# Loads a batch ahead behind a spread that GpSimd issues, query transposes two units earlier, first scores in four visits

## The chip, the cores and the metric

The kernel runs on one core of one Trainium2 chip. Its time is the device time of one execution in microseconds; the figure shown is the median of the runs made. The profile is of one further execution of the same program.

## The reference

Two layers in a row. The first is attention with projected keys and values (8 batches, 8 heads, 1024 tokens, head size 64, 64 projected positions), the second a gated feed-forward network on the 8192 rows that result (512 wide, 1536 hidden).

```python
k_proj = einsum('ks,bhsd->bhkd', E, k);  v_proj = einsum('ks,bhsd->bhkd', F, v)
attn = softmax(q @ k_proj.T / 8)
x = (attn @ v_proj) with heads side by side: 8192 x 512
gate = 1 / (1 + exp(-(x @ w_gate)));  val = x @ w_val
out = (gate * val) @ w_out
```

## The kernel before, in words

All weights stay on the chip. The work goes batch by batch: while the network runs on batch b (two blocks of 512 tokens, each in three thirds of the hidden width, hence six "units" per batch), the attention of batch b + 1 is done in between. All large products are of Strassen's form, seven for eight, and therefore come as chains of small groups: `g_chain` (L1771) and `v_chain` (L1800) once per unit, `o_chain` (L1451) once per block, three units apart. Each chain accumulates in two PSUM banks; ACT copies a bank into the other one as a start (`seed`, L1675) or evacuates it, DVE adds and multiplies.

**What attention of one batch needs**, in the order of its steps:

- K and V (`load_k`, `load_v`, L401 and L411) and Q (`load_q`, L429) are loaded by GpSimd's queue (POOL) from HBM, turned into bf16 on the way, into one buffer each (`KV[0]`, `KV[1]`, `Qb`). A load waits until the buffer's last reader is done: for Q these are the four DMA transposes, for K and V the matmuls of `kv`.
- `next_kv` (L1999): `kv` projects both on PE, `keep_kd` (L896) copies the keys with ACT into `kpd` and lets SP issue one DMA transpose into `kpD` (L910).
- `transpose_q` (L866): SP issues four DMA transposes, r = 0 to 3, two heads each, from `Qb` into `qT` (L870).
- `sc_visit` (L1193): scores of some r on PE, then the exponentials on ACT into `eT`. `den_visit` (L1209): sums of them on PE (`den8`), reciprocals on DVE (`rec`, L977), then `spread`.
- `spread` (L1146): SP writes the reciprocals to DRAM (`rd`, 128 KB, L1149) and, when that has landed, reads them back in four DMAs that repeat each row over 64 partitions (`xu<-rd`, L1165, 512 KB each). The first two are round 0 and serve the first two r, the other two are round 1.
- `xo_visit` (L1201): attention times values on PE, then on DVE the product with the spread, into `xT` (`scaled`, L1182). `xs_sums` makes the sums that the next batch's chains need.

`o_chain` ends in `ost`: ACT evacuates a first quarter early in the chain (`evac`, L1447, shown as L382 with tile `ost`), and at its end SP stores four pieces of 256 KB (`stored`, L1436, L1441). The next block's `evac` may write `ost` only when those stores have landed. After `evac` on ACT come further copies, among them `seed` for the chains that PE works on.

**What sets the order.** For batch 0 and the start of the next the order is written out by hand (`todo`, `put`). From L1992 on, calls of `add` only collect tasks, and `arranged` (L53) makes one order of them: it simulates the engines with fixed costs and takes, among what could start, the task with the earliest due time. A group of matmuls has a goal; unit u of batch b lies at `when(6b + u)`, 9.9 us apart (PACE, L1993), counted from the start of that part. A DMA is counted as 0.6 us of SP or 0.85 us of POOL (L40) and lands after 3.0 us, or after `t` (26 for a load, 8 for a spread). `tie` names keys that a task is to come after, in the plan only: no semaphore is waited on for it. `pad` (default 3.0, SP's tasks alone) is added to what a task waits for, in the plan only. What the program really waits for follows from the keys in `r`, `w` and `x` (L149 to L186). Each engine's queue is then worked off strictly in the order made.

In the main loop (L2022 to L2062), b is the batch of the network and n the attention of batch b + 1. Before the change, batch b starts with `load_k(b + 2)` and `load_v(b + 2)`; for b = 1 visits come one unit later (`late_`). Scores of r = 0, 1 come in unit 0, those of 2, 3 and the sums in unit 1; after them, tied to the spread, `transpose_q` for batch b + 2 and `load_q(b + 3)`, the latter with a real wait for the spread. `next_kv(b + 2)` and the first output visit come in unit 3, the second in unit 4.

Of the kernel before, what the change touches and what calls it, by code (L numbers as in the profile page):

```python
# [116 lines left out]
class Plan:  # L117
# [28 lines left out]
        self.tasks.append(self.open)  # L146
        self.open = None

    def add(self, eng, fn, r=(), w=(), x=(), dma=None, t=None, tie=(), pad=3.0):  # L149
        if self.tasks is not None:  # L150
            self.note(eng, (eng, fn, tuple(r), tuple(w), tuple(x), dma), t, tie, pad)
            return None
        op = Op()
        op.eng, op.fn, op.dma, op.need = eng, fn, dma, False
        op.sem, op.val = None, 0
        deps = {}

        def dep(o, raw):
            if o is op:
                return  # L160
            if o.eng == eng and o.dma is None:
                if eng == "PE" or (eng != "POOL" and not raw):
                    return
            deps[id(o)] = o

        for k in r:
            for o in self.writers.get(k, ()):
                dep(o, True)
        for k in tuple(w) + tuple(x):
# [63 lines left out]
def bass_linformer_attn__then__ffn_glu_sigmoid_kernel(  # L233
# [11 lines left out]
    B = q.shape[0]  # L245
# [6 lines left out]
    with contextlib.ExitStack() as es:  # L252
# [139 lines left out]
        wg_v = moe_w_gate.rearrange("(i p) f -> p i f", p=P)  # L392
        wv_v = moe_w_val.rearrange("(i p) f -> p i f", p=P)

        def load(o, i, w, sem, r=()):
            add("POOL", lambda e: e.dma_start(o, i), r=r, w=w, dma=sem, t=26.0)

        def turned():
            return [("qT", r) for r in range(NR)]

        def load_k(b, after=()):  # L401
            n = 0
            load(
                KV[n][:, :, :],
                k[b].rearrange("h (p t) d -> p h (t d)", t=NT),
                [("KV", n, 0), ("KV", n, 1)],
                f"KV{n}",
                r=(turned() if b >= 2 else []) + list(after),
            )

        def load_v(b):  # L411
            n = 1
            load(
                KV[n][:, :, :],
                v[b].rearrange("h (p t) d -> p h (t d)", t=NT),
                [("KV", n, 0), ("KV", n, 1)],
                f"KV{n}",
            )

        def load_kv_heads(n, src, R):  # L420
# [5 lines left out]
                f"KV{n}{R}",  # L426
            )

        def load_q(b, after=()):  # L429
            load(  # L430
                Qb[:, :, :],
                q[b].rearrange("h (p t) d -> p h (t d)", t=NT),
                [("Q", hf, R) for hf in range(2) for R in range(2)],
                "Q",
                r=after,
            )

        def load_q_half(b, hf, R):
# [424 lines left out]

            return qt, sc, den, bc, xo

        def transpose_q(tie=()):  # L866
            for r in range(NR):
                add(
                    "SP",
                    lambda e, r=r: e.dma_start_transpose(  # L870
                        qT[:, 2 * r : 2 * r + 2, :].rearrange("p h (t c) -> p (h t) c", c=P),
                        Qb[:, 2 * r : 2 * r + 2, :].rearrange("p h c -> p (h c)"),
                    ),
                    r=[("Q", hf, r // 2) for hf in range(2)],
                    w=[("qT", r)] + [("qT", hf, r // 2, r % 2) for hf in range(2)],
                    dma=f"qT{r}",
                    tie=tie,
                )
# [53 lines left out]
        def attention(b):  # L932
# [213 lines left out]
            def spread():  # L1146
# [4 lines left out]
                    w=[("rd", b)],  # L1151
                    dma="rd",
                    t=2.5,
                    pad=0.0,
                )
                for rnd in range(2):
                    for c in range(2):
                        src = (
                            rd_v[b]
                            .rearrange("(g m) (o c) -> o g m c", g=8, o=1)[:, :, 2 * rnd + c, :]  # L1160
                            .to_broadcast([64, 8, 256])
                        )
                        add(
                            "SP",
                            lambda e, src=src, rnd=rnd, c=c: e.dma_start(  # L1165
                                rb[64 * c : 64 * c + 64, rnd, :, :, :].rearrange(
                                    "p j h c -> p (j h) c"
                                ),
                                src,
                            ),  # L1170
                            r=[("rd", b)],
                            w=[("rb", c, rnd), ("spread", c, rnd)],
                            dma=f"rb{c}{rnd}",
                            t=8.0,
                            pad=0.0,
                        )

            def scaled(r, g, bk):
                n = 2 * r + g
# [256 lines left out]
        def stored(blk, tts):  # L1436
            for tt in tts:
# [4 lines left out]
                    r=[("ost", tt, n) for n in range(2)],  # L1442
                    dma=f"out{tt}",
                    t=3.0,
                )

        def evac(bk, tok, col):  # L1447
# [563 lines left out]
        for n in (1, 2, 3, 4):  # L2011
            xs_sums(2, n)
        next_kv(2, -2.0)
        transpose_q()
        t_sums(4)
        t_sums(1)
        o_chain(1, OA, OC, 0.0, 2.0, sums=False)
        for n in (1, 2, 3, 4):
            xs_sums(3, n)

        load_q(3)
        for b in range(1, B):  # L2022
            n = attention(b + 1) if b + 1 < B else None
            if b + 2 < B:
                load_k(b + 2)
                load_v(b + 2)
            late_ = 1 if b == 1 else 0
            for u in range(6):
                K = 6 * b + u
                t0 = when(K)  # L2030
                if n is not None:
                    if u == late_:
                        n["sc_visit"](t0 - 1.0, (0, 1), (GA, GC, XA, XB))
                    if u == late_ + 1:
                        n["sc_visit"](t0 - 1.0, (2, 3), (GA, GC, XA, XB))
                        n["den_visit"](t0 + 3.0, XA)
                        if b + 2 < B:
                            transpose_q(n["spread_keys"])
                        if b + 3 < B:
                            load_q(b + 3, n["spread_keys"])  # L2040
                    if u == late_ + 3:
                        if b > 1 and b + 2 < B:
                            next_kv(b + 2, t0 - 5.0)
                        n["xo_visit"](t0 - 1.0, (0, 1), (GA, GC, XA, XB))
                        if b == 1:
                            next_kv(3, t0 + 4.0)
                    if u == late_ + 4:
                        n["xo_visit"](t0 - 1.0, (2, 3), (GA, GC, XA, XB))
                        for i in (1, 2, 3, 4):
                            xs_sums(2 * b + 2, i)  # L2050
# [46 lines left out]
```

## Time and profile before

| | |
|---|---|
| median of 3 runs | 571.79 us (567.17 to 573.63) |
| the profiled execution's own time | 564.84 us |
| its span, first to last instruction | 563.1 us |
| granted TensorE clock, mean | 0.967 |
| busy share of the span: PE, DVE, ACT, POOL | 91%, 72%, 62%, 7% |
| DMA over the span | 123 GB/s on average; 36.0% of 16 engines' span from POOL's queue, 33.5% from SP's |

In the profile, times are microseconds from the first instruction; "L870" is line 870 of the kernel. SPq and POOLq are queues in which instructions that issue DMAs stand; the length of such an instruction is the time until the queue goes on, not until the data has landed. Where the queue's timeline merges equal instructions (x4), the length reaches from the first one's start to the last one's end. A line of waits tells which engine stood, at which instruction, and what ended it. Nearly all matmuls have one line (L378) and nearly all ACT copies another (L382), so one goes by tiles: pA and pF are PSUM banks.

### The profile page before, as it was taken

To read this page: it belongs to the slowest core of one execution; us is meant where nothing else is said; L and a number is where in the kernel's file an instruction comes from. 1 tells how busy PE (TensorE), PEld (TensorE's weight loads), DVE (VectorE), ACT (ScalarE), POOL (GpSimd) and SP (SyncE) were. 2 spreads that over 40 slices of the span, in tenths; PEclk is the share of its full clock that TensorE was granted. 3 is DMA by queue.
4 is the path that set the end of the run, shared out by engine and by line. 5 is a ranking of instruction groups with operands and counts; after the bars stand their busy time and mean duration, and the time that the engine had idled before them with its cause. 6 is when DMAs were issued, how large, how long until landed. Compare 5 with 4: busy or idle time off the path is not lost.

```text
span 563.1 us, 11315 instructions
## 1 busy us (share of the span) xinstructions
PE 513.1 (91%) x4668; PEld 402.9 (72%) x4677; DVE 405.3 (72%) x670; ACT 351.5 (62%) x644; POOL 37.0 (7%) x52
## 2 busy tenths in 40 slices
PE   5999998798999969999299992999989999999996
PEld 4545546586788858877188781888768888888885
DVE  3648698477886857959168684677777969795964
ACT  2564736575886737874268670587747866667662
POOL 9210200100100010000100001000000000000000
PEclk9999999799999989999599997899989999999999
DMA  9999999958996993179952399822941172010113
GB/s 167 198 201 192 165 223 171 154 139 133 173 201 127 177 218 73 48 105 115 221 97 76 72 113 214 145 76 42 152 127 38 39 162 74 14 63 31 46 39 112
DMA packets 90307, 69.41 MB, mean 123 GB/s; under 512 B 35088, under 2 KB 82448, under 8 KB 90256
## 3 DMA queue, kind: packets, MB, share of 16 engines
q0 software_dynamic: 33984, 29.89, 36.0%
q1 hardware_dynamic: 56272, 38.81, 33.5%
q8 instruction: 36, 0.59, 0.4%
q14 instruction: 15, 0.12, 0.1%
HBM read 72.88 MB, written 17.56 MB: 161 GB/s over the span
## 4 chain that ended last, share of the span: by engine, by line
PE 76%; SPq 9%; DMA 7%; DVE 3%; ACT 2%; issue 1%; POOL 1%; ACTq 0%; DVEq 0%; POOLq 0%
PE pA L378 42%; PE pF L378 34%; SPq L870 8%; DMA out_dram<-ost 2%; DMA KVs<-in_v_dram 2%; DMA xu<-rd 2%; SPq L1441 1%; ACT pF L1678 1%; DMA kpD<-kpd 1%; DVE xT L1182 0%; DVE hT L1811 0%; ACT ost L382 0%; ACT vsnap L382 0%; DVE xT L816 0%; DVE vsnap L1689 0%
## 5 line engine op out<-in xcount | busy, mean ns | idle before, releaser
L382 ACT ACTIVATE sig<-pA 128x512 f32<-128x512 f32 x126 | 75.1, 596 | 49.5 <-PE pA L378 48.4
L1765 DVE TENSOR_TENSOR sig<-pF,sig 128x512 f32<-128x512 f32 x84 | 57.7, 687 | 66.7 <-PE pF L378 38.6
L1689 DVE TENSOR_TENSOR vsnap<-pF,vsnap 128x512 f32<-128x512 f32 x90 | 61.9, 688 | 25.8 <-PE pF L378 14.5
L1678 ACT ACTIVATE pF<-pA 128x512 f32<-128x512 f32 x99 | 58.0, 588 | 32.8 <-PE pA L378 29.8
L378 PE MATMUL pF<-wO,hT 128*128 128x256 bf16 (+1 forms) x400 | 58.8, 285 | 0.2 <-issue 0.2
L1811 DVE SCALAR_TENSOR_TENSOR hT<-sig,vsnap 128x512 bf16<-128x512 f32 x84 | 56.7, 680 | 1.0
L382 ACT ACTIVATE vsnap<-pA 128x512 f32<-128x512 f32 x84 | 50.1, 596 | 8.3 <-PE pA L378 7.2
L382 ACT ACTIVATE sig<-sig 128x512 f32<-128x512 f32 x84 | 52.5, 630 | 4.0 <-DVE sig L1765 3.6
L378 PE MATMUL pF<-xS,wV 128*128 128x256 bf16 x360 | 54.6, 275 | 0.1
L378 PE MATMUL pA<-xS,gT 128*128 128x256 bf16 x168 | 26.4, 282 | 29.2 <-ACT pF L1678 29.2
L378 PE MATMUL pA<-xT,gT 128*128 128x256 bf16 x336 | 51.9, 278 | 0.0
L378 PE MATMUL pF<-xT,wG 128*128 128x256 bf16 (+1 forms) x257 | 50.4, 317 | 1.6 <-DVE hT L1287 0.8
L378 PE MATMUL pF<-xS,wG 128*128 128x256 bf16 x336 | 51.4, 276 | 0.0
L378 PE MATMUL pA<-xT,vT 128*128 128x256 bf16 x336 | 50.5, 273 | 0.0
L378 PE MATMUL pA<-wT,hT 128*128 128x256 bf16 x360 | 49.5, 275 | 0.0
L382 ACT ACTIVATE sig<-pF 128x512 f32<-128x512 f32 x66 | 39.4, 596 | 15.3 <-PE pF L378 13.4
L378 PEld LDWEIGHTS pF<-wO,hT 128*128 128x128 bf16 x402 | 38.5, 98 | 10.3 <-issue 0.8
L378 PEld LDWEIGHTS pF<-xS,wV 128*128 128x128 bf16 x360 | 34.0, 98 | 10.8 <-issue 3.5
L378 PE MATMUL pF<-xT,wV 128*128 128x256 bf16 (+1 forms) x240 | 41.5, 294 | 0.0
L378 PEld LDWEIGHTS pA<-xS,gT 128*128 128x128 bf16 x168 | 15.5, 99 | 34.0 <-ACT pF L1678 30.6
L1811 DVE SCALAR_TENSOR_TENSOR hT<-sig,pF 128x512 bf16<-128x512 f32 x42 | 28.6, 681 | 14.2 <-PE pF L378 12.4
L378 PEld LDWEIGHTS pA<-wT,hT 128*128 128x128 bf16 x360 | 35.4, 99 | 4.7
(152 smaller groups left out, 901.2 us busy)
## 6 DMA issues: line engine op xcount, KB each, us to landing
out_dram<-ost SPq DMA_DIRECT2D x61, 256.0 KB, 2.4
xu<-rd SPq DMA_DIRECT2D x24, 512.0 KB, 11.5
Qb<-in_q_dram POOLq DMA_DIRECT2D x7, 1024.0 KB, 11.2
KVs<-in_k_dram POOLq DMA_DIRECT2D x7, 1024.0 KB, 14.3
KVs<-in_v_dram POOLq DMA_DIRECT2D x7, 1024.0 KB, 20.6
wO<-in_moe_w_out_dram POOLq DMA_DIRECT2D x1, 1536.0 KB, 13.4
wG<-in_moe_w_gate_dram POOLq DMA_DIRECT2D x5, 256.0 KB, 17.5
wV<-in_moe_w_val_dram POOLq DMA_DIRECT2D x5, 256.0 KB, 18.2
```

What stands on the lines that cost most here:

```text
L378: return add("PE", lambda e: e.matmul(o, lhsT, rhs, **kw), r=r, x=[("bank", b)])
L382: return add("ACT", lambda e: e.activation(o, i, func, scale=scale), r=r, w=w, x=x, t=t)
L870: lambda e, r=r: e.dma_start_transpose(qT[:, 2 * r : 2 * r + 2, :].rearrange("p h (t c) -> p (h t) c", c=P), Qb[:, 2 * r : 2 * r + 2, :].r ...
L1441: lambda e, tt=tt, t=t: e.dma_start(out_v[blk // 2, t], ost[:, tt, :]),
L1678: lambda e: e.activation(bank[c][:, :], bank[a][:, :], AF.Copy, scale=1.0),
L1689: lambda e: e.tensor_tensor(o, bank[bk][:, :], o, ALU.add),
L1765: dve(lambda e: e.tensor_tensor(o, bank[bk][:, :], o, ALU.add), [key], [key], b=bk)
L1811: lambda e: e.scalar_tensor_tensor(o, sg.rearrange("p (j c) -> p j c", j=2), 1.0, x.rearrange("p (j c) -> p j c", j=2), ALU.add, ALU.mult,),
```

## The change

It has five parts.

1. The default of `pad` becomes 0.0; only `stored` keeps 3.0.
2. The four reads of the spread are issued by POOL in place of SP. The write of `rd` stays on SP.
3. The loads for batch b + 3 (Q, K, V, in this order, `next_loads`) are issued in batch b at unit 3, tied behind the spread; K waits for both halves of `kpD` as well. For b = 1 they come one unit later. Before, K and V were loaded one batch later. In the start, K of batch 3, V (now with a wait for the transposes) and Q stand together.
4. `transpose_q` for batch b + 2 comes in two halves, right behind the score visits of units 0 and 1, with no tie, for b = 2 to 5. In the start it is tied behind `kpD`. For b = 1 it stays behind the spread.
5. For b = 1 the scores come in four visits of one r each on two banks (XA, XB), with goals 9, 12, 15 and 18 us, and the sums at 21; before, two visits of two r on four banks in units 1 and 2, the sums 3 us into unit 2.

```diff
-    def add(self, eng, fn, r=(), w=(), x=(), dma=None, t=None, tie=(), pad=3.0):
+    def add(self, eng, fn, r=(), w=(), x=(), dma=None, t=None, tie=(), pad=0.0):
...
-        def load_v(b):
+        def load_v(b, after=(), tie=()):
...
+                r=after,
+                tie=tie,
...
-        def transpose_q(tie=()):
-            for r in range(NR):
+        def transpose_q(tie=(), rs=range(NR)):
+            for r in rs:
...
                         add(
-                            "SP",
+                            "POOL",
                             lambda e, src=src, rnd=rnd, c=c: e.dma_start(
...
-        transpose_q()
+        transpose_q([("kpD", 0)])
...
+        load_k(3)
+        load_v(3, turned())
         load_q(3)
+
+        def next_loads(b, marker):
+            if b < B:
+                load_q(b, (), marker)
+                load_k(b, [("kpD", 0), ("kpD", 1)], marker)
+                load_v(b, (), marker)
+
         for b in range(1, B):
             n = attention(b + 1) if b + 1 < B else None
-            if b + 2 < B:
-                load_k(b + 2)
-                load_v(b + 2)
             late_ = 1 if b == 1 else 0
+            more = b + 2 < B
...
-                    if u == late_:
+                    if b == 1 and u == 0:
+                        for r in range(NR):
+                            n["sc_visit"](9.0 + 3.0 * r, (r,), (XA, XB))
+                        n["den_visit"](21.0, XA)
+                        transpose_q(n["spread_keys"])
+                    if b > 1 and u == 0:
                         n["sc_visit"](t0 - 1.0, (0, 1), (GA, GC, XA, XB))
-                    if u == late_ + 1:
+                        if more:
+                            transpose_q((), (0, 1))
+                    if b > 1 and u == 1:
                         n["sc_visit"](t0 - 1.0, (2, 3), (GA, GC, XA, XB))
+                        if more:
+                            transpose_q((), (2, 3))
                         n["den_visit"](t0 + 3.0, XA)
-                        if b + 2 < B:
-                            transpose_q(n["spread_keys"])
-                        if b + 3 < B:
-                            load_q(b + 3, n["spread_keys"])
                     if u == late_ + 3:
-                        if b > 1 and b + 2 < B:
+                        if b > 1 and more:
                             next_kv(b + 2, t0 - 5.0)
+                            next_loads(b + 3, n["spread_keys"])
                         n["xo_visit"](t0 - 1.0, (0, 1), (GA, GC, XA, XB))
                         if b == 1:
                             next_kv(3, t0 + 4.0)
+                            next_loads(4, n["spread_keys"])
```

More of the change, by code (lines that the diff above doesn't have):

```diff
@@ L393, in bass_linformer_attn__then__ffn_glu_sigmoid_kernel, with load, load_k @@
         wv_v = moe_w_val.rearrange("(i p) f -> p i f", p=P)
-        def load(o, i, w, sem, r=()):
-            add("POOL", lambda e: e.dma_start(o, i), r=r, w=w, dma=sem, t=26.0)
+        def load(o, i, w, sem, r=(), tie=()):
+            add("POOL", lambda e: e.dma_start(o, i), r=r, w=w, dma=sem, t=26.0, tie=tie)
         def turned():
             return [("qT", r) for r in range(NR)]
-        def load_k(b, after=()):
+        def load_k(b, after=(), tie=()):
             n = 0
@@ L417, in load_v @@
                 f"KV{n}",
+                r=after,
+                tie=tie,
             )
@@ L427, in load_kv_heads, with load_q @@
             )
-        def load_q(b, after=()):
+        def load_q(b, after=(), tie=()):
             load(
@@ L435, in load_q @@
                 r=after,
+                tie=tie,
             )
@@ L1153, in spread @@
                     t=2.5,
-                    pad=0.0,
                 )
@@ L1174, in spread @@
                             t=8.0,
-                            pad=0.0,
-                        )
+                            )
             def scaled(r, g, bk):
@@ L1444, in stored @@
                     t=3.0,
+                    pad=3.0,
                 )
```

## The prediction

> **What bounds the kernel now.** I read the core's span and clock first, then the waits of PE, the chain around the longest wait, and the SP queue in order of time.
>
> ```profile
> core 0: 563.1 us, clock 0.967
> ```
>
> The waits (engine, line, what was waited for: us in total, times, longest):
>
> ```profile
> ACT ost L382 <- DMA out_dram<-ost: 37.0, 4, 13.4
> ...
> PE pA L378 <- ACT pF L1678: 29.2, 4, 11.4
> ...
> PE pA L378 <- DMA kpD<-kpd: 5.8, 1, 5.8
> ...
> PE pA L378 <- DVE xT L1182: 1.9, 1, 1.9
> ```
>
> From 433 to 543 us PE is busy 110.00 of 110.00 us (last row of the windows below): where nothing stalls it, TensorE's work sets the time. What can be won is its stalls. Four of them, 29.2 us, hang on ACT's seed copy (L1678), and ACT had itself stood four times, 37.0 us, before the evacuation into ost, until the stores of ost had landed. In the second one the last store was issued at 273.47 only (chain: start, us, what), and PE went on at 277.71:
>
> ```profile
> 273.47 3.02 DMA out_dram<-ost
> ...
> 277.71 1.03 PE pA L378 x4
> ```
>
> ```profile
> 276.57 0.60 ACT L382 ACTIVATE ost<-pF 128x512 f32<-128x512 f32 x1 [13.37 <-DMA out_dram<-ost]
> ```
>
> The SP queue (start, us, what) in the first batch, and in the one with that stall:
>
> ```profile
> 88.33 10.82 SPq L870 DMA_TRANSPOSE qT<-Qb  x4
> 99.20 1.29 SPq L910 DMA_TRANSPOSE kpD<-kpd  x1
> ...
> 238.07 0.33 SPq L1149 DMA_DIRECT2D rd<-xu  x1
> 239.78 5.16 SPq L1165 DMA_DIRECT2D xu<-rd  x4
> 249.16 4.43 SPq L910 DMA_TRANSPOSE kpD<-kpd  x1
> 253.69 18.12 SPq L870 DMA_TRANSPOSE qT<-Qb  x4
> 271.91 28.34 SPq L1441 DMA_DIRECT2D out_dram<-ost  x8
> 312.77 0.33 SPq L1149 DMA_DIRECT2D rd<-xu  x1
> ```
>
> The four query transposes hold SP for 18.12 us behind the spread's 2 MB, and the stores of a finished chain stand behind them in the same queue. In the last batch with attention there are no transposes, and the same stores go out in time:
>
> ```profile
> 450.03 0.33 SPq L1149 DMA_DIRECT2D rd<-xu  x1
> 451.73 3.98 SPq L1165 DMA_DIRECT2D xu<-rd  x4
> 462.49 4.68 SPq L1441 DMA_DIRECT2D out_dram<-ost  x4
> ```
>
> A stall costs more than its length, since the granted clock (the third column from the right, after POOL) is low afterwards:
>
> ```profile
> 103.00:113.00 10.00, 10.00 (x83) 8.40 (x80) 6.58 (x12) 7.01 (x14) 0.93 (x2) 0.86 1.08 167
> 203.00:213.00 10.00, 8.94 (x67) 7.40 (x68) 3.90 (x8) 6.73 (x13) 0.00 (x0) 0.83 1.19 194
> 273.00:283.00 10.00, 5.29 (x25) 3.75 (x26) 0.31 (x1) 3.48 (x6) 1.75 (x2) 0.50 1.08 214
> 353.00:363.00 10.00, 10.00 (x85) 8.57 (x83) 5.89 (x11) 6.56 (x12) 0.00 (x0) 0.90 1.13 188
> 413.00:423.00 10.00, 7.83 (x58) 6.16 (x56) 5.89 (x10) 5.01 (x9) 0.00 (x0) 0.83 0.13 48
> 433.00:543.00 110.00, 110.00 (x1027) 95.01 (x1026) 90.07 (x142) 77.43 (x143) 0.00 (x0) 1.00 0.21 60
> ```
>
> Lost to the clock: 1.7 us (0.17 of 10), 2.6 (half of 5.29 busy), about 1.5 (1.0 in its window, 0.5 before it), about 1.3 (1.7 less what lies in the wait): 7 us for the four; 1.4 more in 103 to 113, after the wait for kpD.
>
> **The change part by part.** Durations that the steps need, from issue to landing (KB, median us), the issue of a transpose (ns: least, median, most), and the first product that uses a spread:
>
> ```profile
> out_dram<-ost SPq DMA_DIRECT2D x61, 256.0 KB, 2.4
> xu<-rd SPq DMA_DIRECT2D x24, 512.0 KB, 11.5
> Qb<-in_q_dram POOLq DMA_DIRECT2D x7, 1024.0 KB, 11.2
> KVs<-in_k_dram POOLq DMA_DIRECT2D x7, 1024.0 KB, 14.3
> KVs<-in_v_dram POOLq DMA_DIRECT2D x7, 1024.0 KB, 20.6
> ```
>
> ```profile
> L870 SPq DMA_TRANSPOSE qT<-Qb x28: 1255/3159/9412, 43.3 to 409.8; - x28
> ```
>
> ```profile
> 253.18 0.69 DVE L1182 TENSOR_TENSOR xT<-pA,xu 128x512 bf16<-128x512 f32 x1 [0.27 <-PE pF L378]
> ```
>
> *Transposes to units 0 and 1 (batches 2 to 5).* They go out in pairs as soon as the scores have read qT, before this batch's spread exists; the query has been loaded a batch earlier, so the loads have ended too. Of the three that shared the DMA engines with them (spread, V load, kpD), none is left. A pair then costs SP between 2 x 1.26 = 2.5 us and 9.41 + 4 = 13 us; I take 3 to 6, nearer the low end, as each cause of the long ones is gone. Behind them on SP stand the other pair, rd a unit later, and the stores of the running output chain, which are due only near unit 3, some 20 us on (a unit is 9.9 us): covered even at 13. So the four waits go: **29.2 + 7 = 36 us**.
>
> *What is late next.* The stores at unit 3. In the batch without transposes they issue from 12.5 to 17.1 us after rd and land 2.4 later, at rd + 19.5. ACT wants ost at 276.57 - 13.37 = 263.2, which is rd + 25.1. kpD stays ahead of them on SP: 4.43 us at most here, so rd + 24, still in time. If landing under the loads doubles as well, 1.2 us is missing, four times: 0 to 5 us, and I take 0.
>
> *Spread to POOL.* It removes 5.16 us of issues and the wait for rd's landing (1.4 us: 238.40 to 239.78) from SP. On POOL four issues and that wait stand in front of the next loads only, which have a whole batch of time. The first half of the spread was needed at 253.18, rd + 15.1. From POOL: rd + 1.7, one issue more (0.88, rows below), and 11.5 by the spread's own row or 11.2 by that of a POOL load: rd + 14. That covers it with 1 us to spare. The lower bound is a gain of nothing, as PE had no wait there; the upper one is the slowest POOL load, 20.6 us: rd + 23.2, 8.1 us late in each of six batches. I take 0, since a spread is half of a load's size and now stands ahead of the loads in its queue.
>
> A rule of the Trainium skill speaks against this edit: SBUF — State Buffer, section "SBUF: two separate sides", says that a DMA issued from GpSimd gets its descriptors over the port that it shares with VectorE, so that some VectorE instructions hold it up, and gives 0.62 us alone against 3.1 us beside a copy. In this trace the issue on POOL at 103.05 takes 0.88 us (rows below) while DVE is busy 6.58 us of 10, so no such hold shows in the issue. By that page 2.5 us more on each of four issues would be, as an estimate, 10 us per spread, rd + 24, and in six batches 53 us: about 576 in place of 522.8.
>
> *First batch: kpD ahead of the transposes, the V load behind them, four score visits.* Now:
>
> ```profile
> 86.33 0.88 POOL L396 DMA_DIRECT2D KVs<-in_v_dram  x1 [23.32 <-PE pA L378]
> 102.18 0.87 POOL L396 DMA_DIRECT2D KVs<-in_k_dram  x1 [14.97 <-DMA qT<-Qb]
> 103.05 0.88 POOL L396 DMA_DIRECT2D Qb<-in_q_dram  x1
> ```
>
> The V load runs against the transposes (10.82 us), and kpD, for which PE stands 5.8 us, comes after them. With kpD first and V held back, kpD lands some 10 us earlier, and the scores, now one pair of heads every 3 us, meet their transposes one by one. The same matmuls are issued; with two banks instead of four, each visit waits for the two exponentials before it (about 1.2 us of 3), which covers it. Gain 5.8 + 1.4 = 7.2. Against this the three loads now stand ahead of the first spread in POOL's queue: issued at 96 to 102, landed by the slowest row at 117 to 123, the spread's first half at 125 to 134. Its user ran at 135.4 and would, without the 9.1 us lost before it (5.8, 1.4, 1.9), come at 126.3: a wait of 0 to 8 us where 1.9 was. I take 3, so 1 more than before: **net 6 us**. The transposes of the third batch stay after the spread's place in time, as now.
>
> *Two more waits:* load_k for kpD's landing, the third V load for the transposes; behind both on POOL are only loads that are due a batch later. Pad 0 moves the plan's order alone.
>
> Sum: 36 + 6 = 42 us off the profiled execution's 564.84: 522.8. The median before, 571.79, is 6.95 above that execution, and its single stalls differ from 2.2 to 11.4 us, so I count about half of the difference as stalls that go too, and add 3.5: **526 us**. Its own range: best 44 us and nothing added, 521; worst 42 - 8 - 5 = 29 us and all 6.95 added, 543.
>
> **Rivals.**
> *Half of it.* The stores still come late, behind kpD, whose issue (4.43 us) now meets spread and loads on the other queue. For: kpD was slow whenever the spread ran. Against: the batch at 450 shows 5.6 us of room. If each of the four stalls stays at the mean of the two short ones ((29.2 - 2 x 11.4) / 2 = 3.2 us, with both long ones at 11.4) and about 1.5 of clock, 36 turns into 17, and with 6 the gain is 23: 541.8, on the median 546 to 549.
> *The change doesn't do what it says.* The planner counts a transpose at 0.6 us of SP and may again put both pairs in front of due stores. For: it did so in four batches. Against: in the plan the scores of units 0 and 1 release them two units ahead of the stores. Then the time stays: 566 to 577.
> *Slower: the spread comes late from POOL.* Place: the first output visit of unit 3, where DVE and after it PE stand for the spread in all six batches. It decides from rd + 15.1 on; the gain of 42 is used up at 7 us a batch. At the V load's 20.6 us it is 8.1 x 6 = 49 us: 564.8 - 42 + 49 = 572, on the median 575 to 579. For: 1 us of room by the medians. Against: the 20.6 belongs to the last of three loads issued together, and nothing stands ahead of the spread from batch 2 on.
>
> **How the numbers follow.** The forecast 0.70, half of it 0.13, no effect 0.05, slower 0.09, still faster than 521 us 0.03. A measurement of this kernel tells about 1% from no change. Faster by over 1%: 0.70 + 0.13 + 0.03 = 0.86; within 1%: 0.05; slower: 0.09. The range takes in the forecast's and the half case, with a little room below: 519 to 551.
>
> **What would show it.** Right: SP shows two pairs of transposes per batch ahead of rd, about 3 us each; ACT's wait for stores of ost nearly gone; PE busy 10.00 of 10 from 180 to 540 us at clock 1.00; kpD issued near 87 us; 60 us from one rd to the next, where 74.7 us lie between 238.07 and 312.77 now. Wrong: PE or DVE L1182 waiting for xu<-rd in several batches, transposes still at 4 us and more each, or new waits for qT at unit 0.

## The result, and the profile after

The changed kernel takes 548.45 us (median of 4 runs, 543.53 to 550.96) against 569.48 (4 runs, 566.48 to 573.63): 0.9615 of the time before, with a 95% interval of 0.9514 to 0.9716. It is faster by 21 us; the forecast, 526, lies 43 us below that median. The time lies where the rival "half of it" had put it (546 to 549). The profiled execution took 547.08 us. Executions in a slower state (one of e3's four, one of the kernel before beside e1 to e4) count in the medians of the table below and not in its ratios.

The core's row, the waits (engine, line, what was waited for: us in total, times, longest) and one of ACT's waits in the timeline (start, us, what, in brackets the idle time before it and what ended it), all of the changed kernel:

```profile
core 0: 545.3 us, clock 0.977
```

```profile
PE pA L378 <- ACT pF L1681: 14.6, 3, 5.3
...
PE pA L378 <- DVE xT L1184: 4.9, 1, 4.9
```

```profile
ACT ost L382 <- DMA out_dram<-ost: 22.0, 4, 7.2
```

```profile
268.48 0.60 ACT L382 ACTIVATE ost<-pF 128x512 f32<-128x512 f32 x1 [7.24 <-DMA out_dram<-ost]
```

The wait for kpD is gone. The seed copy (now L1681) still holds PE, three times instead of four and for half as long, and ACT still stands before it until the stores of ost have landed. The SP queue, in the first batch and in the one from rd at 236.11 on, and POOL's queue there (start, us, what):

```profile
87.37 1.74 SPq L914 DMA_TRANSPOSE kpD<-kpd  x1
89.28 5.36 SPq L874 DMA_TRANSPOSE qT<-Qb  x4
...
119.62 20.40 SPq L874 DMA_TRANSPOSE qT<-Qb  x4
```

```profile
230.27 2.62 SPq L874 DMA_TRANSPOSE qT<-Qb  x2
236.11 0.33 SPq L1153 DMA_DIRECT2D rd<-xu  x1
247.20 3.05 SPq L914 DMA_TRANSPOSE kpD<-kpd  x1
250.78 5.97 SPq L1443 DMA_DIRECT2D out_dram<-ost  x4
```

```profile
238.10 2.76 POOL L1168 DMA_DIRECT2D xu<-rd  x4 [42.22 <-DMA rd<-xu]
240.85 0.91 POOL L396 DMA_DIRECT2D Qb<-in_q_dram  x1
```

The transposes are where they were meant to be, 2.62 us a pair. The stores are issued early as well, from rd + 14.7 on. Then they are slow to land. The first fence below is that of these four stores, the second that of the kpD transpose at 247.20, the third that of the four spread reads at 238.10, the fourth that of the query load at 240.85 (from issue to landing):

```profile
DMA to landing us min/median/max: 12.8/13.4/14.2
```

```profile
DMA to landing us min/median/max: 15.8/15.8/15.8
```

```profile
DMA to landing us min/median/max: 8.1/13.1/19.3
```

```profile
DMA to landing us min/median/max: 27.4/27.4/27.4
```

In the kernel before, the stores of the same place were issued at 271.9 to 273.5 and landed in 2.4 to 3.0 us. Now the last one lands at 268.4, rd + 32.3, within 0.2 us of the query load (rd + 32.1). ACT stood ready for `ost` from 268.48 - 7.24 = 261.24 on, rd + 25.1: to the tenth the moment that the prediction had read off. The time is lost in three places (columns as in the prediction: PE busy second, granted clock third from the right); after them PE is full:

```profile
193.00:203.00 10.00, 5.12 (x45) 3.70 (x44) 6.72 (x10) 1.88 (x4) 1.76 (x2) 0.81 1.18 252
203.00:213.00 10.00, 10.00 (x80) 8.43 (x79) 5.59 (x11) 6.48 (x12) 0.00 (x0) 0.85 0.69 116
263.00:273.00 10.00, 4.70 (x29) 3.34 (x27) 4.18 (x7) 2.45 (x5) 1.76 (x2) 0.72 1.19 246
333.00:343.00 10.00, 6.17 (x32) 4.49 (x33) 3.44 (x6) 3.82 (x7) 0.00 (x0) 0.66 1.23 214
360.00:500.00 140.00, 140.00 (x1314) 118.39 (x1312) 115.64 (x182) 100.16 (x185) 5.47 (x8) 1.00 0.33 74
```

From one rd to the next it is 64.4, 68.1 and 67.7 us in these batches. In the first and the third, too, the last store lands with the query load: at rd + 28.8 beside 29.0, and 31.4 beside 31.2. In the next batch, which loads nothing, the stores land by rd + 26.6, no seed copy holds PE, and it is 60.2 us to the next rd.

### The profile page after: what moved, and what is told of

It is laid out like the page before. It is cut to its first block, busy times and chain, and to the rows that moved or that the text cites. A ratio compares the mean times of both kernels' runs of the same rounds, so it can differ in the third digit from the quotient of the medians.

```text
span 545.3 us, 11320 instructions
## 1 busy us (share of the span) xinstructions
PE 512.6 (94%) x4668; PEld 403.1 (74%) x4677; DVE 405.1 (74%) x670; ACT 351.6 (64%) x644; POOL 53.7 (10%) x76
## 4 chain that ended last, share of the span: by engine, by line
PE 80%; DMA 13%; DVE 3%; ACT 1%; issue 1%; POOL 1%; SPq 0%; ACTq 0%; DVEq 0%; POOLq 0%
PE pA L378 44%; PE pF L378 36%; DMA out_dram<-ost 7%; DMA KVs<-in_v_dram 2%; DMA xu<-rd 2%; DMA rd<-xu 1%; DVE hT L1814 1%; DVE vsnap L1692 0%; ACT pF L1681 0%; DVE xT L820 0%; DVE ost L1425 0%; DVE hT L1289 0%; DVE xu L984 0%; POOL KVs L396 0%; POOL Qb L396 0%
## 5 line engine op out<-in xcount | busy, mean ns | idle before, releaser
L1681 ACT ACTIVATE pF<-pA 128x512 f32<-128x512 f32 x99 | 58.2, 589 | 33.5 <-PE pA L378 29.0
L382 ACT ACTIVATE sig<-pF 128x512 f32<-128x512 f32 x66 | 39.4, 596 | 15.3 <-PE pF L378 13.4
L378 PE MATMUL pA<-xS,gT 128*128 128x256 bf16 x168 | 27.1, 287 | 14.6 <-ACT pF L1681 14.6
L1168 POOL DMA_DIRECT2D xu<-rd x24 | 16.5, 702 | 228.6 <-DMA rd<-xu 171.2
L1814 DVE SCALAR_TENSOR_TENSOR hT<-sig,pF 128x512 bf16<-128x512 f32 x42 | 28.7, 683 | 13.6 <-PE pF L378 13.6
L378 PEld LDWEIGHTS pA<-xT,vT 128*128 128x128 bf16 x336 | 31.8, 98 | 9.2 <-ACT sig L382 4.5
## 6 DMA issues: line engine op xcount, KB each, us to landing
wO<-in_moe_w_out_dram POOLq DMA_DIRECT2D x1, 1536.0 KB, 13.1
```

The lines of the kernel that those rows point to most:

```text
L378: return add("PE", lambda e: e.matmul(o, lhsT, rhs, **kw), r=r, x=[("bank", b)])
L382: return add("ACT", lambda e: e.activation(o, i, func, scale=scale), r=r, w=w, x=x, t=t)
L1168: lambda e, src=src, rnd=rnd, c=c: e.dma_start(rb[64 * c : 64 * c + 64, rnd, :, :, :].rearrange("p j h c -> p (j h) c"), src,),
L1681: lambda e: e.activation(bank[c][:, :], bank[a][:, :], AF.Copy, scale=1.0),
L1814: lambda e: e.scalar_tensor_tensor(o, sg.rearrange("p (j c) -> p j c", j=2), 1.0, x.rearrange("p (j c) -> p j c", j=2), ALU.add, ALU.mult,),
```

## The experiments

Each ratio is over the kernel before, run beside it on the same chip; "against the changed kernel" is the difference of two such ratios times 568 us, and carries some 6 us of uncertainty, most of it from the changed kernel's own interval.

| run | what it is | median us | ratio, 95% interval |
|---|---|---|---|
| after | the change | 548.45 | 0.9615 (0.9514 to 0.9716) |
| e1 | all three loads wait for kpD | 525.87 | 0.9262 (0.9212 to 0.9312) |
| e2 | kpD a unit early | 555.74 | 0.9768 (0.9704 to 0.9832) |
| e3 | third query load behind the spread | 553.58 | 0.9715 (0.9637 to 0.9792) |
| e4 | spread back on SP | 562.63 | 0.9923 (0.9885 to 0.9961) |
| e5 | e1 with the spread on SP | 533.82 | 0.9399 (0.9351 to 0.9448) |
| e6 | before, with the transposes moved alone | 551.30 | 0.9694 (0.9640 to 0.9748) |
| e7 | half of each spread read | 532.29 | 0.9366 (0.9327 to 0.9405) |
| e8 | first batch as before | 558.88 | 0.9814 (0.9767 to 0.9860) |
| e9 | e1 with the transposes behind the spread | 563.80 | 0.9925 (0.9888 to 0.9963) |
| e10 | e2, loads wait for the spread | 548.36 | 0.9626 (0.9570 to 0.9682) |

The letters of the theories are those of the expectations. The question was why the stores, issued in time, land late. Two things are new beside them: kpD stands ahead of them on SP, now beside traffic of POOL; and behind the spread on POOL come the loads, the query's at once.

**e1: the loads held back.**

```diff
-                load_q(b, (), marker)
+                load_q(b, [("kpD", 0), ("kpD", 1)], marker)
...
-                load_v(b, (), marker)
+                load_v(b, [("kpD", 0), ("kpD", 1)], marker)
```

> The changed kernel, but the loads of Q and V for batch b + 3 wait for kpD's landing too, as K already does; while kpD and the stores are under way only the spread remains on POOL's queue. Theory A (the stores of ost stand in SP's ring behind kpD's transpose, and that crawls because its 512 small packets take turns with those of POOL's queue until that queue is empty): kpD still shares with the spread and lands about 12 us after its issue, as in the batch at 372 us that has no Q load (11.9), the stores 8 to 9.5 us after theirs in place of 12 to 14; the waits of PE for the seed copy fall from 14.6 to under 4 us, the time by 12 to 18 us (ratio to the changed kernel 0.967 to 0.978). Theory B (plain bandwidth: the Q load takes a share of what moves): the same direction, but kpD lands in 8 us or less. Theory C (the stores are issued late, SP is still held up): no change within 1%.

Measured: 525.87 us, some 20 us less than the changed kernel and the best of all. Core, waits of PE, the two queues of the batch with rd at 228.27, the landing of the stores at 244.04, and the windows' row of the middle of the run:

```profile
core 0: 523.1 us, clock 0.996
```

```profile
PE pA L378 <- DVE xT L1184: 4.4, 1, 4.4
...
PE pA L378 <- ACT pF L1681: 0.6, 1, 0.6
```

```profile
228.27 0.33 SPq L1153 DMA_DIRECT2D rd<-xu  x1
239.36 4.16 SPq L914 DMA_TRANSPOSE kpD<-kpd  x1
244.04 3.88 SPq L1443 DMA_DIRECT2D out_dram<-ost  x4
```

```profile
230.28 2.78 POOL L1168 DMA_DIRECT2D xu<-rd  x4 [40.58 <-DMA rd<-xu]
253.20 0.89 POOL L396 DMA_DIRECT2D Qb<-in_q_dram  x1 [20.14 <-PE pF L378]
```

```profile
DMA to landing us min/median/max: 8.6/9.3/9.8
```

```profile
180.00:500.00 320.00, 319.37 (x2990) 267.94 (x2989) 262.13 (x414) 231.17 (x424) 18.99 (x25) 1.00 0.57 109
```

The query load goes out at 253.20 instead of right behind the spread (this wait is called the gate from here on). The stores still take over three times their undisturbed time, but they have landed by rd + 27.6. ACT stands 2.58 us before `ost` there, until 255.97 (the last store lands at 255.90), where in the other batches with stores in time it stands 1.24 us until PE has filled the bank; PE loses the 0.6 us of the row above. PE is busy 319.37 of 320 us. So a single load of 1 MB beside the stores, once in each of three batches, costs the 20 us, and its data isn't read before long (in the changed kernel 47 us after its issue, by the transposes at 287.82). kpD still took 13.6 us in this batch, as theory A had said and not B; the gain is a little over what either had said.

**e2: kpD out of the way.** `next_kv` moves to unit 1, ahead of the sums; kpD then lands before the spread begins.

```diff
                             transpose_q((), (2, 3))
+                            next_kv(b + 2, t0 + 1.0)
...
-                            next_kv(b + 2, t0 - 5.0)
```

> The changed kernel, but next_kv stands in unit 1, between the second scores and the sums, so that kpD's transpose is issued ahead of the spread; the loads stay tied behind the spread, and K and V now follow at once, so POOL's queue is fuller than before while the stores go out. Theory A (kpD in front of the stores is what holds them): kpD lands in 3 to 4 us, the stores in 5 to 8 us though three loads are under way, PE's waits for the seed copy under 2 us, the time 15 to 22 us less than the changed kernel (ratio 0.96 to 0.973). Theory B (bandwidth of spread and loads): kpD is fast, but the stores still take 12 us or more; the three waits stay or grow, the time is the same or up to 8 us more.

Measured: 555.74 us, some 9 us more than the changed kernel. The kpD transpose issued at 234.1 lands 2.7 us later. The landing of the stores issued from 249.2 on, with no kpD ahead of them:

```profile
DMA to landing us min/median/max: 8.4/12.0/15.7
```

All three loads follow the spread at once in this run. Theory A falls: without kpD ahead of them the stores take 8 to 16 us, not 5 to 8. Theory B comes closer for the stores and right for the time, but it had the waits for the seed copy stay or grow, and they have moved:

```profile
PE pA L378 <- DVE xT L1184: 16.2, 5, 5.5
PE pF L378 <- ACT ost L382: 7.2, 2, 3.8
...
PE pA L378 <- ACT pF L1681: 0.7, 1, 0.7
```

Behind late stores PE now loses 7.2 us (at the evacuation itself) in place of 14.6: issued from rd + 7.5 to 9.5 on, the stores land by rd + 24.5, 28.4 and 29.9 in the three batches, 1.5 to 4.3 us sooner than in the changed kernel. So kpD's place ahead of them did cost something beside the loads. The 16.2 us are waits for the spread, of which the changed kernel has 4.9; e10 shows where they come from. kpD itself is a victim of what is beside it: 2.7 us by itself, 15.8 beside spread and load.

**e3: the third query load behind the first spread.** This is aimed at the 4.9 us that PE waits for the first spread.

```diff
-        load_q(3)
...
+                        load_q(3, (), n["spread_keys"], 10.0)
                         transpose_q(n["spread_keys"])
```

> The changed kernel, but the load of Q for batch 3 stands behind the first spread in POOL's queue, not ahead of it. Theory (the first spread is late because three loads stand ahead of it in its queue): its first half lands some 5 us earlier, the wait of DVE for the spread near 126 us falls from 5.7 to under 1.5 us, the time by 4 to 6 us. Rival (the spread was late because the write of rd took 5.7 us beside the stores, and because of the query transposes that run against it): the wait stays at 3 us or more, the time changes by under 2 us.

(10.0 is what the plan takes as the load's time to landing, in place of 26.) A miss: 553.58 us, not told apart from the changed kernel. The wait for the first spread falls from 4.9 to 2.2 us, so the query load ahead of it was a good part of its cause, but the transposes that need this load then go out against the next batch's spread, 23.09 us for four; the seed waits grow to 18.9 us, and late stores cost another 3.1 in the first batch.

**e4: the spread back on SP, all else as changed.**

```diff
-                            "POOL",
+                            "SP",
                             lambda e, src=src, rnd=rnd, c=c: e.dma_start(
```

> The changed kernel with the four reads of the spread back on SP's queue, all else as changed (the plan then puts the Q load ahead of the spread on POOL, free of it). Theory A: spread, kpD and stores now stand one behind another in one ring; kpD no longer takes turns with the spread, only with the Q load, so the stores land 17 to 21 us after rd, in time as in the last batch with attention; the waits of PE fall to 0 to 6 us, the time by 8 to 18 us. Theory B: the same bytes move at the same time, so the stores land as late as in the changed kernel or, behind the spread in one ring, later: the same time or up to 10 us more. By the prediction, which took the spread on SP to cost 6.6 us of SP per batch under cover: within 1%.

Measured: 562.63 us, some 17 us more than the changed kernel. Both theories missed that, and so did the prediction, which had costed the queue at nothing. PE's waits, and the SP queue of the first batch:

```profile
PE pA L378 <- ACT pF L1681: 15.3, 3, 5.4
PE pA L378 <- ACT vsnap L382: 11.1, 1, 11.1
PE pA L378 <- DVE xT L1184: 8.8, 4, 2.8
```

```profile
110.99 0.33 SPq L1153 DMA_DIRECT2D rd<-xu  x1
116.08 5.10 SPq L1168 DMA_DIRECT2D xu<-rd  x4
121.23 9.75 SPq L1443 DMA_DIRECT2D out_dram<-ost  x4
```

The largest part is one wait of 11.1 us in the first batch, for a copy into `vsnap` that stands behind the evacuation on ACT. SP stands there until rd has landed (5.1 us, beside the loads) and issues the four reads, and only behind them the stores, which land by rd + 28.4 where ACT stood ready from rd + 12.8 on. In the changed kernel the stores of this place are issued from rd + 0.4 on. The waits for the spread take 3.9 us more than in the changed kernel. In the later batches nothing on POOL holds the loads behind the spread now: in the batch with rd at 245.28 the query load goes out at 244.45, ahead of rd, and V at 255.77, and the stores land up to rd + 37. The seed waits are about those of the changed kernel all the same (15.3 and 14.6 us).

**e5: the same with the loads held back** (the edit of e4 on e1).

> The kernel of the first experiment (Q, K and V for the next batch wait for kpD), with the reads of the spread back on SP's queue: nothing of POOL's queue runs beside spread, kpD and stores. Theory D (transposes and stores crawl because their packets take turns with those of the spread or of loads on the other queue; in one queue they follow each other at full speed): the spread lands within 15 to 17 us of rd, kpD 3 to 5 us after it, the stores by rd + 24 to 26; no wait of PE for the seed copy over 1 us, the time that of the first experiment within 1.5%. Theory E (what decides is SP's own queue: four more issues and the wait for rd hold up kpD and the stores): the stores land at rd + 30 or later, waits of 3 us or more come back in three batches, the time is 10 to 20 us over the first experiment.

Measured: 533.82 us, some 8 us more than e1. From batch 2 on it runs as e1 does, 60.4 us from rd to rd. What it lacks is one wait in the first batch, where the stores stand behind the spread in one queue:

```profile
PE pA L378 <- ACT vsnap L382: 10.4, 1, 10.4
```

So once the loads wait, the spread's queue costs nothing in the steady state, about as theory D had said of the time; what the place on POOL is worth is mostly this one wait, 10.4 us here and 11.1 in e4. D's reason doesn't hold: in the batch with rd at 237.05, with nothing on POOL's queue, kpD still took 12.8 us and the stores 7.3 to 9.1, and the spread landed at rd + 22, not 15 to 17. Standing in one queue doesn't make them quick.

**e6: the move of the transposes alone**, on the kernel before, for batches 2 to 5.

```diff
...
+                        if b > 1 and b + 2 < B:
+                            transpose_q((), (0, 1))
...
+                        if b > 1 and b + 2 < B:
+                            transpose_q((), (2, 3))
...
-                        if b + 2 < B:
+                        if b == 1:
                             transpose_q(n["spread_keys"])
```

> The kernel before, with one part of the change alone: for batches 2 to 5 the query transposes come in pairs behind the scores of units 0 and 1; spread on SP, loads and pads as before. By the step of the prediction (the transposes were what held the stores): the four waits go, 30 to 36 us less than before (ratio 0.937 to 0.947). Theory D or E (the stores still stand behind spread and kpD, with K and V loads on the other queue at the same time): only a part, 8 to 20 us less (0.965 to 0.986), with waits for stores of 4 us or more left in most batches.

Measured: 551.30 us, 17.6 less than before. That is what theory D or E had said; the step that the prediction put at 36 us is worth half of that by itself. Two seed waits are left, and the stores, issued from 249.5 on, are as slow as in the changed kernel, beside the spread and the next K and V. PE's waits, and the landing of these stores:

```profile
PE pA L378 <- ACT pF L1678: 15.1, 2, 7.7
```

```profile
DMA to landing us min/median/max: 13.2/13.8/15.3
```

**e7: half the bytes of the spread.** Each read brings 128 of its 256 columns; the other half of the reciprocals is left out.

> The changed kernel, but each of the four reads of the spread brings only half of its columns (256 KB in place of 512 KB); it leaves out the other half, so the second half of each product reads what stood there. The Q load stays right behind the spread. Theory D (the spread's own bytes on POOL's queue set when kpD and the stores get through): spread landed 7 to 9 us earlier, kpD and the stores 6 to 9 us earlier; PE's three waits for the seed copy gone, and the wait for the first spread under 2 us; the time 17 to 24 us less than the changed kernel (0.956 to 0.969 of it). Theory B alone (the Q load is what matters): stores still 10 us or more after their issue, under 8 us gained.

Measured: 532.29 us, some 14 us less than the changed kernel, a little under what theory D had said and more than B. One seed wait is left (6.4 us), and 3.5 us of wait for the first spread. The landing of the four reads issued from 170.1 on, and of those from 230.1 on:

```profile
DMA to landing us min/median/max: 6.0/8.3/11.7
```

```profile
DMA to landing us min/median/max: 8.1/13.8/21.0
```

The first is faster than the whole spread of that batch in the changed kernel (7.0/10.5/14.9), though not twice as fast; the second is no faster than a whole one there (8.1/13.1/19.3). So bytes alone don't set these times.

**e8: the first batch as before** (transposes ahead of kpD, V load beside them, two visits in units 1 and 2).

```diff
-        transpose_q([("kpD", 0)])
+        transpose_q()
...
-        load_v(3, turned())
+        load_v(3)
...
```

(and the two visits in place of the four)

> The changed kernel with the start as before: the transposes of batch 2 ahead of kpD, the V load beside them, the scores of batch 2 in two visits of two r on four banks in units 1 and 2. By the prediction, whose net for this part was 6 us, and by the profile (5.8 us of wait and 1.4 of clock won, 3 more lost at the first spread): the wait for kpD of 5 to 6 us is back, the wait for the first spread 1 to 3 us; 3 to 6 us more than the changed kernel. Rival (the smaller visits cost what the earlier kpD brings): the same time within 2 us.

Measured: 558.88 us, some 11 us more than the changed kernel (0.020 of the time before, give or take 0.011), more than the 3 to 6 that were expected. The wait for kpD is back (5.5 us), that for the first spread is 9.0, and the seed waits are 17.1. The third batch's transposes go out at rd + 1.5 here, in place of rd + 9.0, and stand 29.09 us on SP beside the spread (20.40 in the changed kernel).

**e9: e1 with the transposes back behind the spread.** This asks whether the move is needed once the loads wait.

```diff
-                        if more:
-                            transpose_q((), (0, 1))
...
-                        if more:
-                            transpose_q((), (2, 3))
                         n["den_visit"](t0 + 3.0, XA)
+                        if more:
+                            transpose_q(n["spread_keys"])
```

> The kernel with the loads held back until kpD has landed (the run of 525.9), with the move of the query transposes undone for batches 2 to 5: all four stand behind the spread again, and so behind kpD on SP. It asks what the move is worth once no load runs beside the stores. Theory D (what SP sends beside POOL's traffic gets through about when that traffic has landed): kpD lands some 13 us after its issue as in that run, only then do the transposes issue; the V load starts at the same moment, so they take 3 to 5 us each, and the stores behind them are issued 12 to 20 us later than without them, some 30 to 35 us after rd and land later still, where ACT wants them at rd + 25 to 28: the seed waits come back in four batches, 4 to 10 us each with their share of the clock, 545 to 565. Rival F (holding the loads back is all that counts, the transposes cost their 3.2 us each and the slack takes them up): within 5 us of the run without this edit, 524 to 531, and no seed wait over 2 us.

Measured: 563.80 us, some 38 us more than e1. F falls; D holds in the waits and the time, though the stores are issued sooner than its rd + 30 to 35. PE's waits and the SP queue behind rd, at 237.18:

```profile
PE pA L378 <- ACT pF L1681: 30.9, 4, 10.9
```

```profile
...
252.00 10.17 SPq L874 DMA_TRANSPOSE qT<-Qb  x4
262.27 2.97 SPq L1443 DMA_DIRECT2D out_dram<-ost  x4
```

The stores are issued at rd + 25.1, when ACT wants them landed. They take 10.6 to 10.9 us, beside the V load that kpD's landing has let go. Both edits are needed: neither the move on the kernel before (e6, 17.6 us) nor the changed kernel with the gate and without the move (e9, some 4) brings half of what e1 brings, some 42.

**e10: kpD early, and the loads behind the landed spread.** Only the spread is left beside the stores.

```diff
-                load_q(b, (), marker)
+                load_q(b, marker, marker)
...
-                load_v(b, (), marker)
+                load_v(b, marker, marker)
```

(and K's wait in the same way)

> The kernel that issues kpD a unit early (the run of 555.7), with the three loads of the next batch now waiting for the landing of all four parts of the spread, instead of standing right behind them in the queue. Beside the stores runs the spread alone, and no kpD stands ahead of them. Theory D: the spread, alone with the stores, lands by rd + 13 to 16 (rd + 23 in the changed kernel) and the stores with it or earlier, by rd + 14 to 18, far ahead of rd + 25; no seed wait, no wait of DVE for the spread from batch 2 on, rd to rd 60 to 61: 523 to 531. Theory G (the stores are late by themselves, whenever the spread runs beside them, and the gate of the run of 525.9 helped for another reason, its kpD standing ahead): stores still 11 to 15 us after issue and seed waits of 10 us and more in all, 540 to 556.

Measured: 548.36 us, 8 us less than e2, and a miss for both theories. PE's waits, then the landing of the four spread reads issued from 239.9 on, and of the stores from 247.4 on (rd at 237.93):

```profile
PE pA L378 <- DVE xT L1184: 18.4, 5, 5.0
```

```profile
DMA to landing us min/median/max: 8.9/13.7/20.2
```

```profile
DMA to landing us min/median/max: 7.0/11.2/15.3
```

The spread, with the stores alone beside it, takes 20.2 us; that goes against theory D. The stores are about as slow as G said, yet they land by rd + 26.4, and the seed wait is gone (0.7 us, and 1.5 at the evacuation), as D said. The time falls in G's range for another reason, the waits for the spread. Of their 18.4 us, 5.0 lie in the first batch, as in the changed kernel. The rest is the price of kpD's early place, as in e2: the plan now has the first output visit ask for the spread at rd + 10.0, when its first half lands at rd + 14.4:

```profile
252.46 0.69 DVE L1184 TENSOR_TENSOR xT<-pA,xu 128x512 bf16<-128x512 f32 x1 [4.49 <-DMA xu<-rd]
```

In e1 the same product runs at 243.38, rd + 15.1, and doesn't wait for the spread.

## Why the prediction was partly right

The forecast of 526 was missed by 22 us, and the prediction's own range for it, 521 to 543, as well; 519 to 551 holds the time only because it takes in the rival "half of it".

*What bounds the kernel: right.* TensorE is full wherever nothing stalls it (140.00 of 140 us from 360 to 500). The stalls were the seed copies behind late stores, and the kernel that removes them (e1) comes out at 525.87 us with the clock at 0.996.

*Transposes to units 0 and 1: right in itself.* A pair costs 2.6 us (3 to 6 were taken) and the stores come out early. All four waits were to go; that hung on the next step.

*What is late next: this step failed.* It had the stores issued from rd + 12.5 to 17.1, with kpD's issue ahead up to 4.43 us later (measured: 14.7 to 19.1), wanted at rd + 25.1 (measured: 25.1), and landing 2.4 us after issue, or double that at worst. They took 12.8 to 14.2 and landed up to rd + 32.3. The 2.4 us was a median over 61 stores, wherever they stood. The row of the batch at 450, taken as evidence of room, had a spread but no load beside its stores, and even there the trace before shows more than 2.4 us for them:

```profile
DMA to landing us min/median/max: 3.6/4.8/6.0
```

The step asked when SP would issue the stores, not what else would be in flight then, and the change itself puts a load there. The mis-sized term is 0 to 5 us for four batches, where 14.6 us of waits were measured and, counted from the windows as the prediction did, about 6 us of clock (0.19 of 5.12, 0.15 of 10, 0.28 of 4.70, 0.34 of 6.17).

*"Half of it": right in size, half right in its reason.* It had the stores late behind kpD's issue on SP. That issue is 3.05 us and needn't cost anything: e1 keeps kpD there and loses 0.6 us. With the loads in flight kpD's place does count: without it the stores land 1.5 to 4.3 us sooner (e2), and still too late in two batches. The rival's size came from the short waits of the kernel before, so that its 546 to 549 fits is luck.

*Spread to POOL: taken at 0, and no wait for it came from batch 2 on, as said.* But undoing it in e4 costs some 17 us, so its worth was underrated. The prediction named what the edit takes off SP, four issues and the wait for rd, and gave it no price; in e4 and e5 the stores of the first batch stand behind just these, and PE loses 11.1 and 10.4 us. Of the port rule (the Trainium skill, SBUF — State Buffer, "SBUF: two separate sides") nothing shows: POOL issued the four reads in 2.76 us, and the 576 us estimated by that rule did not come. Another rule of the Trainium skill would have spoken against the edit as well: DMA: Bandwidth & Descriptors, "SWDGE vs HWDGE vs iDMA", concludes that plain transfers belong on SP or ACT. Here they are better on POOL, by 17 us without the gate and by 8 with it.

*First batch: 6 us said, 3 to 4 found between the two profiles.* kpD's wait went (issued at 87.37, "near 87" was said); the first spread's wait was 4.9, where 3 was taken and 0 to 8 allowed. By the prediction's way of counting, 5.8 + 1.9 us of waits and 1.4 of clock became 4.9 and 0.6 (0.11 of 5.11 from 123 to 133). Taken back alone (e8), the part is worth some 11 us: besides the wait for kpD, the first spread is 4.1 us later than in the changed kernel and the seed waits are 2.5 longer. What was not counted is that with the old start the third batch's transposes go out against the spread, at rd + 1.5 (rd + 7.7 in the kernel before).

*Mechanism.* Shown is what the loads beside the stores cost. With kpD ahead of the stores they end at rd + 28.8, 32.3 and 31.4 with the query load in flight, and at 21.4, 27.6 and 24.5 without it (the changed kernel and e1); with no kpD ahead, at 24.5, 28.4 and 29.9 with the three loads and at 20.6, 26.4 and 24.4 without them (e2 and e10). In e1 PE loses 0.6 us where they end at rd + 27.6; in the changed kernel, at rd + 28.8 and later, 4.4 to 5.3 us a batch. They don't wait for all that is in flight: in e2 they land some 13 us ahead of the last load. Why these transfers slow each other down is only argued. The Trainium skill (DMA: Bandwidth & Descriptors, "Queues, rings and completion order") has each DMA engine serve its queues in turn, a packet at a time. The packet records of the changed kernel would fit: kpD makes 512 packets of 256 B, four stores 512 of 2 KB, so 1024 on SP in turn with some 576 of the spread and 1024 of a load of 1 MB, and the stores end when the query load does. But three things are not explained by queues that take turns: in e5, with nothing on POOL's queue, kpD and the stores are about as slow as in e1; e7's half spread lands no sooner in one batch; and e10's spread needs 20.2 us with four stores alone beside it. That stays open.

## What to carry to other kernels

A DMA's landing time belongs to a place in the schedule, not to its kind: take it from a row with the same neighbours in flight, and when a change moves transfers, list what will be in flight beside each one that someone waits for. Transfers that are needed only most of a batch later should wait for a late event, the landing of the urgent ones, and not merely stand behind them in a queue: here that wait, two lines, was worth as much as the whole change. A queue that works in order and stands waiting holds up all that stands behind it: the spread's reads on SP cost one wait of 10 to 11 us at the single place where stores came behind them. Two edits that each clear one obstacle from the same path may bring little one by one: the move alone stops at 551, the changed kernel with the gate and without the move at 564, and with both it reaches 526.

## What the runs showed of the hardware that was not expected

The same 24 reads of 512 KB make different packets by the queue that issues them. The rows of the queues (packets, MB, share of 16 engines' span), before and then after:

```profile
q0 software_dynamic: 33984, 29.89, 36.0%
q1 hardware_dynamic: 56272, 38.81, 33.5%
```

```profile
q0 software_dynamic: 37440, 42.47, 50.3%
q1 hardware_dynamic: 43600, 26.22, 21.1%
```

The 12.58 MB that moved are 12672 packets on SP's queue (528 a read) and 3456 on POOL's (144 a read). Beside other traffic an SP transfer can take five times as long and more: stores 2.4 us against 12.8 to 14.2, kpD 2.7 against 15.8. The Trainium skill (Advanced Engine Details and Errata, "DMA Advanced Topics") calls transpose DMAs as fast as others. The trace doesn't quite agree: with little beside it, kpD's 128 KB take 2.7 us (e2) and the plain write of rd, as many bytes, 1.7; beside the spread kpD took 13.6 us in e1 and the stores, of twice its bytes, 8.6 to 9.8.
